# A list schedule that keeps one clock for all of SyncE's loads and stores, in a fused attention and SwiGLU kernel

## The chip, the cores and the metric

One core of a Trainium2 chip runs the whole kernel. The metric is device time in microseconds (us), the median of a few runs of the same program. TensorE does the matmuls, ScalarE (ACT) and VectorE (DVE) copy, round and add, GpSimd (POOL) takes some of that, and SyncE (SP) issues nearly all DMAs.

## The reference

Retention attention over 4 sequences of 768 tokens and 8 heads of 64, in blocks of 64 tokens with a carried state; then one SwiGLU layer over the 3072 token rows of 512:

```python
intra = (qb @ kb.T * Dmask) @ vb
inter = (qb * lam_pow) @ kv_state
out[:, :, sl] = intra + inter
kv_state = lam_block * kv_state + (kb * rev_pow).T @ vb
...
xn = x / sqrt(mean(x * x) + 1e-6) * rms_g
g = xn @ w_gate                       # 512 x 1536
return (silu(g) * (xn @ w_val)) @ w_out
```

All inputs and the output are float32. Matmuls of the SwiGLU part run as three float16 products each (high by high, low by high, high by low).

## The kernel before

The 3072 tokens are 6 groups m of 512, the 1536 hidden columns are 12 blocks f of 128, so there are 72 units (m, f), numbered u. The first 24 units (`classical`) are two plain products, gate and value, on weights that lie in the on-chip tile `w_half`. While they run, weights are converted to float16 pairs, sums of weight blocks are made and written out to `gw_kept` in DRAM. Units 24 to 71 (`strassen`) make the same two products out of seven smaller ones, and each of them first reads its weights back: `gv` (256 KB, three buffers) and `gw` (640 KB, two buffers). The two buffers of `gw` mean that a unit's load can't start before the last matmul on `gw` two loads earlier is over. In the names of the order below, `pa_3_1` and `pb_3_1` are the two accumulators of group 3, block 1, which is unit 37; `gw_37` is that unit's weights. A unit's result `sg` is stored in `h_kept`, read back later as `h`, and multiplied with the output weights (`o`, lines 924 and 1029). Attention of a coming group (`pa` at line 478, `po` at 539 and 550, on `qkv`) is woven in between.

Nothing of this order is written by hand. Each piece of work is a step with an engine, an estimated duration, a wished place `at`, and the names it reads and writes. `Plan.run` (lines 1110 to 1207) takes the steps one by one: it holds a clock per engine and picks the step that could start first. The recorded order is then the program order on each engine. `SHIFTS` (line 1691 on) is a table that moves the wished place of some steps, each named by its number. DMAs are steps too. Before, they were four separate engines with a clock each:

```python
ENGINES = ("PE", "ACT", "DVE", "POOL", "LD", "LO", "LH", "ST")
...
step("LO", 0.7, u - 1.6, load_val, u, f, r=[f"gk{f}:b"], w=[wv], new=[(wv, "gv")], lasts=1.8)
step("LO", 1.75, u - 1.59, load_others, u, f, r=[f"gk{f}:b", f"gk{f}:s", wv], w=[w], new=[(w, "gw")], lasts=1.8)
```

LD loads inputs, LO loads weights, LH loads rows and output weights, ST stores. A step of cost c and `lasts` l is taken to be finished c + l after its start. In the program all of these are DMAs of the one SyncE queue, in the order in which the plan placed them, and a DMA that must wait holds back those behind it.

Of the kernel before, what the change touches and what calls it, by code (L numbers as in the profile page):

```python
# [18 lines left out]
G = 512  # L19
# [3 lines left out]
def retention_swiglu_kernel(  # L23
# [754 lines left out]
    class Hidden:  # L778
# [38 lines left out]

        def keep(self, t):
            nc.scalar.copy(self.val_sums[:, t * HG : (t + 1) * HG], self.pa)  # L819

        def sum_val(self, t):
            v = self.val_sums[:, t * HG : (t + 1) * HG]
            nc.vector.tensor_add(v, self.pb, v)  # L823

        def keep_gate(self):
            self.sg = tmp.tile([P, G], F32, tag="t", name=f"sg_{self.m}_{self.f}")
            nc.scalar.copy(self.sg[:, HG:], self.pa)  # L827

        def sum_gate(self):
            nc.vector.tensor_add(self.sg[:, HG:], self.pb, self.sg[:, HG:])  # L830

        def silu_half(self, t):
            half = slice(t * HG, (t + 1) * HG)
            nc.scalar.activation(
                self.sg[:, half], self.sg[:, half] if t else self.pa, AF.Silu,
                scale=cg[:, self.f, 0:1],
            )

        def mul_sums(self, t=None):
            half = slice(0, G) if t is None else slice(t * HG, (t + 1) * HG)  # L840
# [102 lines left out]
    class Operands:  # L943
# [13 lines left out]
        def sums(self, part):  # L957
            if self.hs:
                (a11, a21), (a12, a22) = (
# [21 lines left out]
        def parts(self, n):  # L981
# [6 lines left out]
            if n == 0:  # L988
                return self.hs[0].sg[:, :HG], to[:, 0, 0], to[:, 0, 1]
# [70 lines left out]
    class Plan:  # L1060

        ENGINES = ("PE", "ACT", "DVE", "POOL", "LD", "LO", "LH", "ST")
# [41 lines left out]
        @staticmethod  # L1104
        def lag(a, b):
            if a == b:
                return 0.0 if a == "PE" else 0.03
            return 0.22 if a == "PE" else 0.1 if a in ("LD", "LO", "LH", "ST") else 0.06

        def run(self, horizon=1.3, reach=900):  # L1110
# [44 lines left out]
            while left:  # L1155
                for limit in (horizon, 99.0):
                    found = {e: [] for e in self.ENGINES}
                    for i in left[:reach]:
                        eng, _, at = steps[i][:3]
                        if at > progress + limit or eng in self.LOADS and found[eng]:  # L1160
# [6 lines left out]
                    found = {e: sorted(x for x in c if x[1] < 1e9) for e, c in found.items()}  # L1167
# [21 lines left out]
                start, eng, i = best  # L1189
                _, cost, at, _, _, r, w, new, lasts = steps[i]  # L1190
                clock[eng] = start + cost - self.NEXT.get(eng, 0.0)
# [91 lines left out]
    def out_weight_steps(j, at):  # L1283
# [3 lines left out]
        for i in range(2):  # L1287
            f = 2 * j + i
            step("LH", 1.4, at - 1.0 + 0.1 * i, load_o, f, w=[f"ro{f}"], new=[(f"ro{f}", "raw_o")], lasts=1.8)
# [10 lines left out]
        step("ST", 0.05, at + 0.65, o.keep, r=both, w=[f"wk{j}"], lasts=4.0)  # L1300
# [4 lines left out]
    def out_sum_steps(o, at):  # L1305
# [3 lines left out]
        step("LH", 1.4, at - 1.0, o.load, r=[f"wk{j}"], w=[b], new=[(b, "w")], lasts=1.8)  # L1309
# [5 lines left out]
    def block_steps(m, j, at, d):  # L1315
# [3 lines left out]
        step("LH", 1.4, at - 0.7, o.load, r=[f"hk{n}:0", f"hk{n}:1"], w=h, new=[(f"hp{n}", "w")], lasts=1.8)  # L1319
# [5 lines left out]
    def plain_rows_steps(m, at, length):  # L1325

        for i in range(2):
# [8 lines left out]
            for t in range(2):  # L1336
                key = f"ro{m}_{i}_{t}"
                step("ACT", 0.66, at + length * (i + 1) / 2 - 1, r.keep, t, r=[banks[t], "ik"], w=[key], new=[(key, "o")])
                step("ST", 0.05, at + length * (i + 1) / 2 - 1, r.send, t, r=[key], w=[f"sent{key}"], lasts=4.0)

    def sum_steps(f, at):
        s = WeightSums(f)
        both = [f"wg{f}", f"wv{f}", room_of(f)]
        step("ST", 0.1, at - 0.5, s.send_blocks, r=both, w=[f"gk{f}:b"], lasts=4.0)
# [9 lines left out]
        step("ST", 0.05, at + 1.3, s.send, r=[f"ws16_{f}"], w=[f"gk{f}:s"], lasts=4.0)  # L1354
# [198 lines left out]
    def strassen(u, h):  # L1553
# [8 lines left out]
        step("LO", 0.7, u - 1.6, load_val, u, f, r=[f"gk{f}:b"], w=[wv], new=[(wv, "gv")], lasts=1.8)  # L1562
        step("LO", 1.75, u - 1.59, load_others, u, f, r=[f"gk{f}:b", f"gk{f}:s", wv], w=[w], new=[(w, "gw")], lasts=1.8)
# [36 lines left out]
    def room_step(i, at):  # L1600
        step("ST", 0.0, at, late_room, i, new=[(f"late{i}", f"big{i}")], w=[f"late{i}:c{j}" for j in range(3)])

    def operand_steps(m, j, at, d):
# [7 lines left out]
        else:  # L1611
            h = [[f"hp{n}:{i}"] for i in range(2)]
            step("LH", 1.4, at - 0.7, o.load, r=[f"hk{n}:0", f"hk{n}:1"], w=[f"hp{n}:0", f"hp{n}:1"],
                 new=[(f"hp{n}", "w")], lasts=1.8)
# [19 lines left out]
    def rows_steps(m, at, length):  # L1634
# [5 lines left out]
        for k, n in enumerate(PHASES):  # L1640
# [13 lines left out]
            if n in to:  # L1654
# [3 lines left out]
                step("ST", 0.05, t, r.send, c, i, j, r=[f"late0:c{c}"], w=[f"sent{m}_{k}"], lasts=4.0)  # L1658
# [13 lines left out]
    def load_steps():  # L1672
        queue = [(1, 0), 1, 2, (1, 1), 3, (1, 2), 4, (1, 3), *range(5, NF)]
        queue += [(m, p) for m in range(2, NG) for p in range(NP)]
        for key in queue:
            if isinstance(key, tuple):
# [6 lines left out]
                step("LD", 2.8, -9, load_qkv, m, p, w=[f"{name}:{c}" for c in "qKkv"], new=[(name, "in")], lasts=1.8)  # L1683
            else:
                step("LD", 2.8, -9, load_gv, key, w=[f"gv{key}"], new=[(f"gv{key}", "in")], lasts=1.8)

    SHIFTS = {
# [252 lines left out]
```

## Time and profile before

| | us |
|---|---|
| median of 3 runs | 700.91 (698.31 to 705.19) |
| the profiled execution, own time | 704.38 |
| its span, first to last instruction | 702.6 |
| TensorE busy in the span | 653.7 (93%) |
| VectorE busy | 490.3 (70%) |
| mean granted clock of TensorE | 0.983 |

A busy TensorE is one that has a matmul in flight, not one at its full rate: the next matmul of a row starts before the last one has left. What a row costs is read from start to start, or from long merged rows. "Waited for" is idle time that ended when the thing named was done.

### The profile page before, as it was taken

The numbers are of one execution on the slowest core, as the hardware profiler recorded it, in microseconds if no ns is written. First come the engines' busy times: TensorE is split into PE (matmuls) and PEld (weight loads), VectorE is DVE, ScalarE is ACT, GpSimd is POOL, SyncE is SP. The second block draws the span as 40 slices with busy tenths as digits, with TensorE's granted clock in tenths as the row PEclk, the third lists the DMA queues.
The fourth block names the chain that finished last, engine by engine and source line by source line (L and its number), as shares of the span: only waits on it lengthen the run. The fifth ranks groups of instructions, "written<-read, shape, count | busy, mean of one in ns | idle before, by whom it ended". The sixth has DMA issues, their size and how long they took to land.

```text
span 702.6 us, 14209 instructions
## 1 busy us (share of the span) xinstructions
PE 653.7 (93%) x5667; PEld 494.4 (70%) x5667; DVE 490.3 (70%) x925; ACT 374.4 (53%) x696; POOL 136.7 (19%) x109
## 2 busy tenths in 40 slices
PE   8999999999979996998896989899999999999997
PEld 7865444445646764766674878788789888888886
DVE  6778977899899882776573738875665825854760
ACT  3669665965447551655564535564654424534630
POOL 2222600044553773120000301200121200000000
PEclk9999999999999998999998999999999999999999
DMA  8676499648676387757765554654864646442501
GB/s 321 220 248 244 168 366 350 230 148 269 237 258 210 123 293 274 244 167 251 253 219 199 191 208 166 215 183 140 275 209 127 196 145 210 169 140 76 195 16 46
DMA packets 58594, 144.06 MB, mean 205 GB/s; under 512 B 6176, under 2 KB 23072, under 8 KB 57120
## 3 DMA queue, kind: packets, MB, share of 16 engines
q1 hardware_dynamic: 58384, 142.64, 59.3%
q8 instruction: 44, 0.72, 0.4%
q10 hardware_dynamic: 144, 0.52, 0.3%
q14 instruction: 22, 0.18, 0.1%
HBM read 106.96 MB, written 36.18 MB: 204 GB/s over the span
## 4 chain that ended last, share of the span: by engine, by line
PE 62%; DMA 20%; DVE 9%; ACT 4%; issue 3%; SPq 1%; POOL 0%; DVEq 0%; ACTq 0%; POOLq 0%
PE o L1029 17%; PE pa L770 13%; PE pb L770 10%; DMA gw<-gw_kept 6%; PE pv L659 5%; PE pg L659 4%; DMA h_kept<-sg 4%; DMA h<-h_kept 4%; DMA gv<-gw_kept 3%; PE pa L478 2%; PE po L539 2%; PE o L924 2%; PE po L550 2%; PE pst L511 1%; PE pss L592 1%
## 5 line engine op out<-in xcount | busy, mean ns | idle before, releaser
L770 PEld LDWEIGHTS <-gw 128*128 128x128 f16 x1440 | 140.5, 99 | 49.1 <-DMA gw<-gw_kept 20.9
L1029 PE MATMUL o<-wo,late 128*128 128x256 f16 x1260 | 149.5, 273 | 0.0
L1029 PEld LDWEIGHTS <-late 128*128 128x128 f16 x1260 | 122.8, 98 | 15.5 <-issue 0.5
L659 PEld LDWEIGHTS <-w_half 128*128 128x128 f16 x576 | 54.1, 98 | 68.8 <-issue 6.2
L770 PE MATMUL pa<-tx,gw 128*128 128x256 f16 x576 | 79.5, 278 | 16.4 <-DMA gw<-gw_kept 15.3
L819 ACT COPY tx<-pa 128x256 f32<-128x256 f32 x96 | 35.4, 371 | 91.7 <-PE pa L770 82.2
L823 DVE TENSOR_TENSOR tx<-pb,tx 128x256 f32<-128x256 f32 x96 | 40.1, 421 | 48.7 <-PE pb L770 39.1
L770 PEld LDWEIGHTS <-gv 128*128 128x128 f16 x576 | 57.2, 101 | 20.2 <-DMA gv<-gw_kept 10.3
L659 PE MATMUL pv<-x,w_half 128*128 128x512 f16 x288 | 67.5, 379 | 2.8 <-DVE sg L851 1.6
L659 PE MATMUL pg<-x,w_half 128*128 128x512 f16 x288 | 67.9, 383 | 0.3 <-ACT w_half L440 0.3
L502 POOL TENSOR_TENSOR qkv<-qkv,pw 128x512 f32<-128x512 f32 x24 | 32.9, 1373 | 175.0 <-PE pa L478 162.6
L830 DVE TENSOR_TENSOR sg<-pb,sg 128x256 f32<-128x256 f32 x48 | 20.1, 422 | 50.7 <-ACT sg L827 49.3
L770 PE MATMUL pa<-x,gv 128*128 128x256 f16 x288 | 41.4, 282 | 9.6 <-DMA gv<-gw_kept 9.6
L999 DVE TENSOR_TENSOR late<-s,late 128x1024 f16<-128x1024 f32 x30 | 38.0, 1272 | 9.5 <-ACT late L995 9.5
L770 PE MATMUL pb<-tx,gw 128*128 128x256 f16 x288 | 40.3, 279 | 2.6 <-DMA gw<-gw_kept 2.1
L770 PE MATMUL pb<-x,gw 128*128 128x256 f16 x288 | 39.0, 272 | 2.7 <-DVE sg L830 2.6
L770 PE MATMUL pb<-x,gv 128*128 128x256 f16 x288 | 41.0, 281 | 0.0
L770 PE MATMUL pa<-x,gw 128*128 128x256 f16 x288 | 39.0, 272 | 0.0
L720 POOL TENSOR_TENSOR ws<-ws,ws 128x512 f16<-128x512 f32 x24 | 30.3, 1274 | 41.9 <-ACT ws L716 29.2
L995 ACT CAST late<-s 128x1024 f16<-128x1024 f32 x30 | 31.1, 1045 | 11.4 <-DVE s L979 8.1
L924 PE MATMUL o<-wo,early 128*128 128x512 f16 x144 | 35.6, 382 | 0.0
L498 DVE TENSOR_TENSOR a<-pa,mask 128x512 f32<-128x512 f32 x48 | 31.4, 684 | 5.7 <-PE pa L478 3.6
(147 smaller groups left out, 1071.2 us busy)
## 6 DMA issues: line engine op xcount, KB each, us to landing
gw<-gw_kept SPq DMA_DIRECT2D x48, 640.0 KB, 4.5
qkv<-in_qkv_dram SPq DMA_DIRECT2D x47, 512.0 KB, 6.3
h<-h_kept SPq DMA_DIRECT2D x30, 512.0 KB, 4.5
gv<-gw_kept SPq DMA_DIRECT2D x48, 256.0 KB, 4.9
raw_gv<-in_weights_dram SPq DMA_DIRECT2D x11, 1024.0 KB, 6.6
h_kept<-sg SPq DMA_DIRECT2D x60, 128.0 KB, 4.9
h_kept<-sg SPq DMA_DIRECT2D x30, 256.0 KB, 4.7
raw_o<-in_weights_dram SPq DMA_DIRECT2D x24, 256.0 KB, 4.3
```

Source lines behind the costliest of these rows:

```text
L498: nc.vector.tensor_mul(self.a[:, j], self.pa[j], decay)
L502: eng.tensor_mul(self.qT, self.qT, pw[:, p : p + 1, :].broadcast_to([P, GC, P]))
L659: nc.tensor.matmul(ps, w[:, kk, :], x[:, kk, :], start=i == kk == 0, stop=i == 2 and kk == NK - 1,)
L720: eng.tensor_sub(self.to[:, c, 1], self.t[:, c], self.to[:, c, 0])
L770: nc.tensor.matmul(ps, w(ow, k), x(ox, k), start=first and i == k == 0, stop=i == 2 and k == 1, skip_group_check=True,)
L819: nc.scalar.copy(self.val_sums[:, t * HG : (t + 1) * HG], self.pa)
L823: nc.vector.tensor_add(v, self.pb, v)
L830: nc.vector.tensor_add(self.sg[:, HG:], self.pb, self.sg[:, HG:])
L924: nc.tensor.matmul(self.banks[t], h[:, oh, t * P : (t + 1) * P], wo[:, j, 3 + 2 * k : 5 + 2 * k, ow], start=j == k == i == 0, stop=j == HA ...
L995: nc.scalar.copy(hi, of)
L999: eng.tensor_sub(lo, of, hi)
L1029: nc.tensor.matmul(bank[:, t], ops[:, oh, t * P : (t + 1) * P], w[:, ow], start=n in (1, 2, 5) and q == t == i == 0, stop=q == HALF - 1 an ...
```

## The change

Work, tiles and arithmetic stay. Three things differ.

First, the plan: LD, LO, LH and ST share one clock, `SP`, and their costs and `lasts` are larger. A load of `gw` was finished 1.75 + 1.8 = 3.55 us after its start and is now finished after 2.4 + 2.8 = 5.2, a load of `gv` after 1.0 + 2.8 = 3.8 in place of 2.5; stores, which cost 0.05, now hold the clock for 0.8 to 1.55. Steps that only open a tile go to a clock of their own, `ROOM`, where they cost nothing.

Second, `SHIFTS` is another table (one line of each stands below).

Third, for units 24 and up the two halves of `sg` with an even f are kept in the order in which they are stored, so that `keep_h` is one DMA of 256 KB where it was two of 128 KB. The program has 359 DMA issues on SyncE where it had 377.

```diff
-        ENGINES = ("PE", "ACT", "DVE", "POOL", "LD", "LO", "LH", "ST")
+        ENGINES = ("PE", "ACT", "DVE", "POOL", "SP", "ROOM")
+
+        SP = ("LD", "LO", "LH", "ST")
...
+        def half(self, t):
+
+            t = t if self.f % 2 else 1 - t
+            return slice(t * HG, (t + 1) * HG)
...
-            if self.f % 2:
-                nc.sync.dma_start(to[:, 1], self.sg)
+            if self.f % 2 or self.u >= 2 * NF:
+                nc.sync.dma_start(to[:, self.f % 2], self.sg)
...
-        @staticmethod
-        def lag(a, b):
+        def lag(self, a, b):
+            if a in self.SP:
+                return 0.1
...
-                            found[eng].append((at, t, i))
-                        elif eng in self.LOADS:
-                            found[eng].append((at, 1e9, i))
+                            found["SP" if eng in self.SP else eng].append((at, t, i))
+                        if eng in self.LOADS:
+                            seen.add(eng)
...
-                clock[eng] = start + cost - self.NEXT.get(eng, 0.0)
+                if cost:
+                    clock[unit] = start + cost - self.NEXT.get(eng, 0.0)
...
-        step("ST", 0.05, u - 1, h.keep_h, r=[f"sg{u}:0", f"sg{u}:1", f"sg{u}"], w=[f"hk{h.m}_{h.f // 2}:{h.f % 2}"],
-             lasts=4.0)
+        step("ST", 0.8, u - 1, h.keep_h, r=[f"sg{u}:0", f"sg{u}:1", f"sg{u}"], w=[f"hk{h.m}_{h.f // 2}:{h.f % 2}"],
+             lasts=2.0)
...
-        step("LO", 0.7, u - 1.6, load_val, u, f, r=[f"gk{f}:b"], w=[wv], new=[(wv, "gv")], lasts=1.8)
-        step("LO", 1.75, u - 1.59, load_others, u, f, r=[f"gk{f}:b", f"gk{f}:s", wv], w=[w], new=[(w, "gw")], lasts=1.8)
+        step("LO", 1.0, u - 1.6, load_val, u, f, r=[f"gk{f}:b"], w=[wv], new=[(wv, "gv")], lasts=2.8)
+        step("LO", 2.4, u - 1.59, load_others, u, f, r=[f"gk{f}:b", f"gk{f}:s", wv], w=[w], new=[(w, "gw")], lasts=2.8)
...
-                step("LD", 2.8, -9, load_qkv, m, p, w=[f"{name}:{c}" for c in "qKkv"], new=[(name, "in")], lasts=1.8)
+                step("LD", 3.7, -9, load_qkv, m, p, w=[f"{name}:{c}" for c in "qKkv"], new=[(name, "in")], lasts=2.8)
...
-        2709: 6.123, 2715: 5.968,
...
+        2637: 8.777, 2641: 4.085, 2656: 1.098, 2675: -2.059, 2701: 1.816, 2716: 1.22,
```

The order changes nearly everywhere on all five engines. Two places show what the prediction rests on.

TensorE, from the last use of the buffer that `gw_39` needs to the first matmul on `gw_39` (unit 39 is group 3, block 3). Before, that buffer was `gw_37`'s; between any two rows that are shown stand more matmuls of the same kind, six to a product:

```order
L770 MATMUL pb_3_1_3796<-x_3_2440,gw_37_3681 128x256
...
L770 MATMUL pa_3_0_3763<-x_3_2440,gw_36_3751 128x256
...
L770 MATMUL pb_3_0_3778<-x_3_2440,gw_36_3751 128x256
...
L770 MATMUL pa_3_2_3966<-x_3_2440,gv_38_3804 128x256
...
L770 MATMUL pb_3_2_3974<-x_3_2440,gv_38_3804 128x256
...
L770 MATMUL pa_3_3_3985<-x_3_2440,gv_39_3708 128x256
...
L770 MATMUL pb_3_3_3996<-x_3_2440,gv_39_3708 128x256
...
L770 MATMUL pa_3_3_3985<-tx_0_2178,gw_39_3954 128x256
```

In the change the buffer was `gw_35`'s, and the load stands in the queue right behind that of `qkv_4_2`, which needs `po_4_0` finished (line 550):

```order
L770 MATMUL pb_2_11_3642<-x_2_1918,gw_35_3651 128x256
...
L550 MATMUL po_4_0_3784<-qkv_4_0_2995,state_170 64x128 x6
...
L770 MATMUL pb_3_1_3815<-x_3_2376,gv_37_3631 128x256
...
L770 MATMUL pa_3_2_3828<-x_3_2376,gv_38_3773 128x256
...
L770 MATMUL pa_3_1_3757<-tx_0_2101,gw_37_3739 128x256
...
L1034 MATMUL o_1_1_3862<-wo_178,late0_3578 128x256
...
L770 MATMUL pb_3_1_3815<-x_3_2376,gw_37_3739 128x256
...
L1034 MATMUL o_1_2_3920<-wo_178,late0_3578 128x256
...
L770 MATMUL pa_3_3_3964<-x_3_2376,gv_39_3789 128x256
...
L770 MATMUL pa_3_3_3964<-tx_0_2101,gw_39_3879 128x256
```

Before, 36 matmuls of 128x256 lie between the release and the use. In the change the rest of unit 37, products of `o` and attention's scores of the next pair have moved in between.

SyncE, in the stretch of the queue with the loads of units 38 to 41. Before:

```order
L736 DMA gw_39_3954<-gw_kept3_100 128x2560
L736 DMA gw_38_3981<-gw_kept2_99 128x2560
L862 DMA h_kept3_0_133<-sg_3_0_3928 128x256 x2
L858 DMA h_kept3_0_133<-sg_3_1_3845 128x512
L731 DMA gv_41_4006<-gw_kept5_102 128x1024
L951 DMA h_1_5_4049<-h_kept1_5_126 128x1024
L736 DMA gw_41_4074<-gw_kept5_102 128x2560
L96 DMA qkv_4_3_4093<-in_qkv_dram 128x1024 x2
L731 DMA gv_40_4097<-gw_kept4_101 128x1024
```

And in the change:

```order
L736 DMA gw_39_3879<-gw_kept3_100 128x2560
L96 DMA qkv_4_3_3916<-in_qkv_dram 128x1024 x2
L956 DMA h_1_4_3961<-h_kept1_4_125 128x1024
L864 DMA h_kept3_0_133<-sg_3_1_3905 128x512
L736 DMA gw_38_4000<-gw_kept2_99 128x2560
L731 DMA gv_40_4032<-gw_kept4_101 128x1024
L956 DMA h_1_5_4043<-h_kept1_5_126 128x1024
L864 DMA h_kept3_0_133<-sg_3_0_3702 128x512
```

`gv_40` stood right behind the 1 MB load of `qkv_4_3`; now three rows, a load of `gw` among them, lie between the two, and the store of `sg_3_0` is one row of 128x512 without the mark x2.

## Rows read from the trace of the kernel before

**Rows 1.** The page: span, then busy time of engines with share and instruction count.

```profile
span 702.6 us, 14209 instructions
...
PE 653.7 (93%) x5667; PEld 494.4 (70%) x5667; DVE 490.3 (70%) x925; ACT 374.4 (53%) x696; POOL 136.7 (19%) x109
```

**Rows 2.** Stretches of 50 us: busy time by engine, granted clock, DMA share, GB/s.

```profile
150.00:200.00 50.00, 46.09 (x363) 25.49 (x362) 46.12 (x83) 24.21 (x36) 25.15 (x21) 0.98 0.72 242
200.00:250.00 50.00, 46.63 (x416) 32.39 (x414) 44.52 (x80) 30.26 (x50) 28.42 (x21) 0.98 0.57 202
...
350.00:400.00 50.00, 41.90 (x400) 34.68 (x400) 32.40 (x60) 25.83 (x49) 4.01 (x3) 0.93 0.58 194
...
500.00:550.00 50.00, 49.27 (x498) 42.37 (x496) 33.19 (x62) 27.89 (x57) 9.01 (x6) 1.00 0.63 206
```

**Rows 3.** What TensorE waited for: us in total, times, longest us.

```profile
PE pa L770 <- DMA gw<-gw_kept: 15.3, 9, 5.8
PE pa L770 <- DMA gv<-gw_kept: 9.6, 2, 6.5
...
PE pb L770 <- DMA gw<-gw_kept: 2.1, 1, 2.1
```

**Rows 4.** Timeline of TensorE, 354 to 384 us: start, length, what, idle before.

```profile
359.68 0.82 PE L770 MATMUL pb<-x,gv 128*128 128x256 f16 x6
361.85 0.83 PE L770 MATMUL pa<-tx,gw 128*128 128x256 f16 x6 [1.35 <-DMA gw<-gw_kept]
...
371.19 0.57 PE L511 MATMUL pst<-qkv 128*64 128x64 f32 x12
378.22 1.46 PE L770 MATMUL pa<-x,gv 128*128 128x256 f16 x6 [6.46 <-DMA gv<-gw_kept]
```

**Rows 5.** Timeline of SyncE, 354 to 384 us: DMA issues, start and length.

```profile
368.62 0.81 SPq L96 DMA_DIRECT2D qkv<-in_qkv_dram  x2
369.48 0.42 SPq L731 DMA_DIRECT2D gv<-gw_kept  x1
```

**Rows 6.** Tile gw: its loads.

```profile
DMA to landing us min/median/max: 3.7/4.5/9.1
```

**Rows 7.** Tile gv: its loads.

```profile
DMA to landing us min/median/max: 2.7/4.9/9.0
```

**Rows 8.** Tile qkv: its loads.

```profile
DMA to landing us min/median/max: 3.8/6.3/9.5
```

**Rows 9.** Four stretches in which the granted clock was half: columns as in rows 2.

```profile
266.60:273.40 6.80, 4.50 (x20) 3.00 (x21) 0.03 (x1) 0.74 (x2) 0.00 (x0) 0.50 0.89 345
341.70:345.10 3.40, 3.40 (x19) 2.39 (x16) 0.42 (x1) 2.28 (x5) 0.00 (x0) 0.51 1.02 373
375.80:382.60 6.80, 4.38 (x21) 3.14 (x22) 1.46 (x5) 1.10 (x4) 0.00 (x0) 0.50 0.26 96
413.30:416.70 3.40, 2.78 (x14) 1.99 (x15) 0.00 (x0) 0.37 (x1) 0.00 (x0) 0.50 0.10 39
sum 20.40, PE 15.06 PEld 10.52 DVE 1.92 ACT 4.50 POOL 0.00; mean PE 3.76 PEld 2.63 DVE 0.48 ACT 1.12 POOL 0.00
```

**Rows 10.** Chain that ended last: start, length, piece.

```profile
157.44 2.59 PE pg L659 x12
...
197.15 7.22 DMA h_kept<-sg
204.39 3.66 DMA h<-h_kept
...
213.90 6.11 DMA h<-h_kept
...
672.51 26.21 PE o L1029 x240
```

**Rows 11.** What SyncE's DMA queue waited for: us in total, times, longest us.

```profile
SPq L1048 <- DVE late L1042: 67.4, 11, 16.7
```

More of the change, by code (lines that the diff above doesn't have):

```diff
@@ L816, in add @@
             )
+        def half(self, t):
+            t = t if self.f % 2 else 1 - t
+            return slice(t * HG, (t + 1) * HG)
         def keep(self, t):
-            nc.scalar.copy(self.val_sums[:, t * HG : (t + 1) * HG], self.pa)
+            nc.scalar.copy(self.val_sums[:, self.half(t)], self.pa)
         def sum_val(self, t):
-            v = self.val_sums[:, t * HG : (t + 1) * HG]
+            v = self.val_sums[:, self.half(t)]
             nc.vector.tensor_add(v, self.pb, v)
@@ L826, in keep_gate @@
             self.sg = tmp.tile([P, G], F32, tag="t", name=f"sg_{self.m}_{self.f}")
-            nc.scalar.copy(self.sg[:, HG:], self.pa)
+            nc.scalar.copy(self.sg[:, self.half(1)], self.pa)
         def sum_gate(self):
-            nc.vector.tensor_add(self.sg[:, HG:], self.pb, self.sg[:, HG:])
+            g = self.sg[:, self.half(1)]
+            nc.vector.tensor_add(g, self.pb, g)
         def silu_half(self, t):
-            half = slice(t * HG, (t + 1) * HG)
+            half = self.half(t)
             nc.scalar.activation(
@@ L839, in mul_sums @@
         def mul_sums(self, t=None):
-            half = slice(0, G) if t is None else slice(t * HG, (t + 1) * HG)
+            half = slice(0, G) if t is None else self.half(t)
             sg = self.sg[:, half]
@@ L1157, in run @@
                     found = {e: [] for e in self.ENGINES}
+                    seen = set()
                     for i in left[:reach]:
                         eng, _, at = steps[i][:3]
-                        if at > progress + limit or eng in self.LOADS and found[eng]:
+                        if at > progress + limit or eng in seen:
                             continue
@@ L1163, in run @@
                         if t is not None:
[L1164 to L1167 removed]
+                            found["SP" if eng in self.SP else eng].append((at, t, i))
+                        if eng in self.LOADS:
+                            seen.add(eng)
+                    found = {e: sorted(c) for e, c in found.items()}
                     if any(found.values()):
@@ L1188, in run @@
                         best = start, eng, pick[2]
-                start, eng, i = best
-                _, cost, at, _, _, r, w, new, lasts = steps[i]
-                clock[eng] = start + cost - self.NEXT.get(eng, 0.0)
+                start, unit, i = best
+                eng, cost, at, _, _, r, w, new, lasts = steps[i]
+                if cost:
+                    clock[unit] = start + cost - self.NEXT.get(eng, 0.0)
                 end[i] = start + cost + lasts
@@ L1288, in out_weight_steps @@
             f = 2 * j + i
-            step("LH", 1.4, at - 1.0 + 0.1 * i, load_o, f, w=[f"ro{f}"], new=[(f"ro{f}", "raw_o")], lasts=1.8)
+            step("LH", 1.9, at - 1.0 + 0.1 * i, load_o, f, w=[f"ro{f}"], new=[(f"ro{f}", "raw_o")], lasts=2.8)
             step("ACT", 0.67, at + 0.2 * i, o.lift, i, r=[f"ro{f}"], w=[f"{b}:{i}"],
@@ L1299, in out_weight_steps @@
         w = f"wo{j}"
-        step("ST", 0.05, at + 0.65, o.keep, r=both, w=[f"wk{j}"], lasts=4.0)
+        step("ST", 1.55, at + 0.65, o.keep, r=both, w=[f"wk{j}"], lasts=2.0)
         step("ACT", 1.1, at + 0.65, o.high, 0, r=both, w=[f"{w}:0", f"{w}:1"])
@@ L1308, in out_sum_steps @@
         b, w, t = f"wog{j}", f"wo{j}:1", f"wt{j}"
-        step("LH", 1.4, at - 1.0, o.load, r=[f"wk{j}"], w=[b], new=[(b, "w")], lasts=1.8)
+        step("LH", 1.9, at - 1.0, o.load, r=[f"wk{j}"], w=[b], new=[(b, "w")], lasts=2.8)
         step("DVE", 0.84, at, o.sums, 0, r=[b], w=[t], new=[(t, "raw_o")])
@@ L1318, in block_steps @@
         h = [f"hp{n}:{i}" for i in range(2)]
-        step("LH", 1.4, at - 0.7, o.load, r=[f"hk{n}:0", f"hk{n}:1"], w=h, new=[(f"hp{n}", "w")], lasts=1.8)
+        step("LH", 1.9, at - 0.7, o.load, r=[f"hk{n}:0", f"hk{n}:1"], w=h, new=[(f"hp{n}", "w")], lasts=2.8)
         for i in range(2):
@@ L1338, in plain_rows_steps @@
                 step("ACT", 0.66, at + length * (i + 1) / 2 - 1, r.keep, t, r=[banks[t], "ik"], w=[key], new=[(key, "o")])
-                step("ST", 0.05, at + length * (i + 1) / 2 - 1, r.send, t, r=[key], w=[f"sent{key}"], lasts=4.0)
+                step("ST", 0.8, at + length * (i + 1) / 2 - 1, r.send, t, r=[key], w=[f"sent{key}"], lasts=2.0)
     def sum_steps(f, at):
@@ L1343, in sum_steps @@
         both = [f"wg{f}", f"wv{f}", room_of(f)]
-        step("ST", 0.1, at - 0.5, s.send_blocks, r=both, w=[f"gk{f}:b"], lasts=4.0)
+        step("ST", 1.2, at - 0.5, s.send_blocks, r=both, w=[f"gk{f}:b"], lasts=2.0)
         for i in range(2):
@@ L1353, in sum_steps @@
             step("POOL", 1.15, at + 1.1 + 0.05 * i, s.low, i, r=[f"ws{f}"], w=[f"ws16_{f}"])
-        step("ST", 0.05, at + 1.3, s.send, r=[f"ws16_{f}"], w=[f"gk{f}:s"], lasts=4.0)
+        step("ST", 1.55, at + 1.3, s.send, r=[f"ws16_{f}"], w=[f"gk{f}:s"], lasts=2.0)
     def classical(u, h, columns=None):
@@ L1600, in room_step @@
     def room_step(i, at):
-        step("ST", 0.0, at, late_room, i, new=[(f"late{i}", f"big{i}")], w=[f"late{i}:c{j}" for j in range(3)])
+        step("ROOM", 0.0, at, late_room, i, new=[(f"late{i}", f"big{i}")], w=[f"late{i}:c{j}" for j in range(3)])
     def operand_steps(m, j, at, d):
@@ L1612, in operand_steps @@
             h = [[f"hp{n}:{i}"] for i in range(2)]
-            step("LH", 1.4, at - 0.7, o.load, r=[f"hk{n}:0", f"hk{n}:1"], w=[f"hp{n}:0", f"hp{n}:1"],
-                 new=[(f"hp{n}", "w")], lasts=1.8)
+            step("LH", 1.9, at - 0.7, o.load, r=[f"hk{n}:0", f"hk{n}:1"], w=[f"hp{n}:0", f"hp{n}:1"],
+                 new=[(f"hp{n}", "w")], lasts=2.8)
             if m <= UNSCALED:
@@ L1657, in rows_steps @@
                     step("DVE", 0.74, t, r.sum, c, r=[names[False], "ik"], w=[f"late0:c{c}"])
-                step("ST", 0.05, t, r.send, c, i, j, r=[f"late0:c{c}"], w=[f"sent{m}_{k}"], lasts=4.0)
+                step("ST", 0.8, t, r.send, c, i, j, r=[f"late0:c{c}"], w=[f"sent{m}_{k}"], lasts=2.0)
     FACTORS = 23
@@ L1682, in load_steps @@
                 name = f"q{m}_{p}"
-                step("LD", 2.8, -9, load_qkv, m, p, w=[f"{name}:{c}" for c in "qKkv"], new=[(name, "in")], lasts=1.8)
+                step("LD", 3.7, -9, load_qkv, m, p, w=[f"{name}:{c}" for c in "qKkv"], new=[(name, "in")], lasts=2.8)
             else:
-                step("LD", 2.8, -9, load_gv, key, w=[f"gv{key}"], new=[(f"gv{key}", "in")], lasts=1.8)
+                step("LD", 3.7, -9, load_gv, key, w=[f"gv{key}"], new=[(f"gv{key}", "in")], lasts=2.8)
     SHIFTS = {
[97 rows of a table removed]
[125 rows of a table added]
     }
@@ L1840, in retention_swiglu_kernel @@
                     norm_steps(m + 1, u, 0.2)
-        step("ST", 0.0, START[0] - 3, early_room, new=[("early", "big0")], w=["early:"])
+        step("ROOM", 0.0, START[0] - 3, early_room, new=[("early", "big0")], w=["early:"])
         for m in range(PLAIN):
```

6 lines of the change are left out of this document (3 added, 3 removed), and 221 rows, old and new, of the table SHIFTS.

## The prediction

> **What bounds the kernel now.** I read the page first: TensorE has a matmul in flight in 653.7 of 702.6 us, VectorE is busy in 490.3 [rows 1]. So TensorE is the engine to follow, and a gain must come from its idle time or from time in which it runs below its rate. The windows of 50 us say where that is [rows 2]: it is idle for 3.9 and 3.4 us between 150 and 250 us, for 8.1 between 350 and 400, and hardly at all at 500 to 550. Between 150 and 250 VectorE is busy in 46.12 and 44.52 of 50 us, so there it is close to being the bound; from 350 on it has a third of its time free.
>
> Third, what TensorE waits for [rows 3]. The waits for the weight loads of the units with seven products stand out: 15.3 + 9.6 + 2.1 = **27.0 us** in 12 waits, the longest 5.8 and 6.5. The timeline shows one of each kind [rows 4]: 1.35 us for `gw` at 361.85, and 6.46 us for `gv` at 378.22. The queue shows why the second is so long [rows 5]: `gv` is issued at 369.48, directly behind the two halves of a `qkv` load of 1 MB that started at 368.62, and lands only when TensorE goes on, 8.7 us later.
>
> Fourth, the clock. After the long waits stand four stretches at 0.50 of the granted clock, the lower of the two levels, 1.2 GHz for 2.4 [rows 9]: six matmuls took 1.46 us behind the wait of 6.46 and 0.83 behind the one of 1.35 [rows 4]. In these 20.40 us TensorE was busy for 15.06, and half of that, **7.5 us**, would not have been needed at the upper level. The Trainium skill (TensorE: Matmul & The Clock Gate, Terms) counts the penalty as the whole throttled time by one minus the share of the clock. By that the four stretches cost 10.2 us, because it counts the idle part of them too; the sum below goes by the busy part.
>
> **What the change moves, and the price of each part.** A 128x256 matmul costs 26.21 / 240 = 0.109 us in a long row, a 128x512 one 2.59 / 12 = 0.216 [rows 10]. With these prices I count in the order the TensorE work between what a load must wait for (the free buffer, and all that the queue's rows ahead of it wait for) and the first matmul on the load; call it the load's room. For `gw_39` before it is 36 matmuls, 3.9 us; in the change 12.8. The queue needs 4.5 us from issue to landing for `gw`, 3.7 at best and 9.1 at worst [rows 6], and 4.9, 2.7 and 9.0 for `gv` [rows 7]. A room of 3.9 us is thus nearly always too small, and that is what the old plan gave: it took 3.55 us for granted. Over all 48 units the rooms of `gw` are:
>
> - before: 8 at 3.9, 25 under 6.0, the middle one 5.9;
> - in the change: none under 5.7, 7 under 6.0, the middle one 7.9.
>
> For `gv` the least grows from 3.0 to 5.2, and those under 6.0 fall from 4 to 2. The loads of `qkv`, which land after 6.3 us in the middle [rows 8], had 6 rooms under 6.0 (least 3.0) and now none under 7.2. No kind of load has lost its room.
>
> *Waits for `gw` and `gv`*: 27.0 us go. What is left? Upper bound: each old wait stays, less the growth of the tight rooms, 2.0 for `gw` (3.9 to 5.9) and 2.2 for `gv` (3.0 to 5.2). 5.8 becomes 3.8, the eight others of that row, 1.2 each, vanish, 2.1 becomes 0.1, 6.5 becomes 4.3 and 3.1 becomes 0.9: 9.1 us. Lower bound: that, scaled by the tight loads of both kinds, 9 for 29: 2.8 us. I take 6.0, the middle, since the worst landings (9.1, 9.0) are beyond the new middle rooms.
>
> *Half speed*: 7.5 us go. If the two longest waits stay as in the upper bound, their stretches stay, (4.50 + 4.38) / 2 = 4.4 us [rows 9]; if not, nothing. I take 2.4.
>
> *The stage of 150 to 250 us.* Here TensorE's chain runs through stores and loads of the hidden rows: `h_kept` 7.22 us, `h` 3.66, `h` again 6.11 [rows 10]. The least room of an `h` load grows from 5.9 to 9.0. The first matmul on a `gv` load also comes after 9.6 us less TensorE work (199.3 for 208.9), which only moves that work behind it. VectorE stays nearly full, so of the 7.3 us that TensorE idles here I take 3.0 as gained; bounds 0 and 7.3.
>
> *Stores of `sg`*: 18 DMA issues fewer, at about 0.4 us each on the queue [rows 5], 7 us of SyncE. They are covered: SyncE is waiting for others in far more than that, 67.4 us for the output rows alone [rows 11]. Nothing for TensorE. The new halves of `sg` change which columns are written, not the size of a step: nothing. `ROOM` issues nothing. Filler matmuls in the first stage are 43 for 51; they stand in waits, so nothing (at most 2 us).
>
> Sum: 704.4 - 27.0 - 7.5 + 6.0 + 2.4 - 3.0 = 675.3 us for the profiled execution's own time. That execution stands 3.5 us above the median of its runs, so I scale by 700.91 / 704.38: **672 us**, 4.1% faster.
>
> **The rivals.**
>
> *The load waits are only a cover (688 us).* With TensorE no longer held up, VectorE and ScalarE meet it with less lead. The old waits gave them time to catch up; for this speaks VectorE's 46.12 of 50 [rows 2], against it the third of its time that is free from 350 us on, where most of the load waits are. If half of the net gain on loads (27.0 + 7.5 - 6.0 - 2.4 = 26.1) comes back as waits for them and the early stage gives nothing, 704.4 - 13.0 = 691.4, scaled 688.
>
> *All of it goes (659 us).* No load is late, the half-speed stretches vanish, and the early stage loses its 7.3 us too: 704.4 - 34.5 - 7.3 = 662.6, scaled 659. The worst landings speak against it.
>
> *No change (701 us).* The loads could land later just because they are issued earlier, into the same 1 MB transfers, so that more room buys nothing. Rows 6 speak against it: nearly all landings lie between 3.7 and 9.1, and it is the room that was short. Here belongs a rule of the Trainium skill (DMA: Bandwidth & Descriptors, Anatomy of one DMA, given for the gpsimd path): 2.0 us and the bytes by 436 GB/s. By it a `gw` load of 640 KB takes 3.5 us, the old plan's 3.55 was right, a room of 3.9 held every load, and the change could give nothing at all, 701 us. The trace disagrees, 4.5 in the middle [rows 6]. That a larger plan cost moved nothing, so that the change would not do what it says, is out: the rooms in the order have grown.
>
> *Slower (715 us).* One row of SyncE holds back all behind it. A store of output rows waits 67.4 / 11 = 6.1 us for VectorE [rows 11]. My rooms count TensorE's work only: if VectorE is late, a `gw` load behind such a store is issued 6.1 us later, the middle room leaves 7.9 - 4.5 = 3.4, and TensorE waits 2.7 us. Ten such loads eat up the gain of 27.0; with 16 of them and the old load waits and half speed gone it is 704.4 - 29.1 + 43.2 = 718.5, scaled 715. For it: in the new order 44 of the 96 loads of `gv` and `gw` stand right behind a store, in the old one 36. Against: the old order had nearly as many, and its waits came where rooms were small, as at 361.85.
>
> **How the numbers follow.** Forecast (662 to 684): 0.52. Half comes back (684 to 694): 0.19. All goes (under 662): 0.15. No change: 0.08. Slower: 0.06. The three runs shown lie within 1%, so I count 1% as what can be told from no change. Faster by more than that, under 693.9: 0.52 + 0.19 + 0.15 = 0.86; within 1%: 0.08; slower: 0.06. The range reaches from just below the case in which all goes, 657, to 694, the edge of the one in which half comes back; about 0.05 lies below it and 0.14 above. The forecast's own range is 662 to 684.
>
> **What would show it.** In the list of TensorE's waits, `gw` and `gv` together between 3 and 9 us instead of 27.0. Stretches at half clock behind load waits: two or fewer, with the window of 350 to 400 above 0.93. The landing times of `gw` about as before, 4.5 in the middle: then the room did it; if they fall to 3.7, the transfers got faster and the step is another. In the windows from 150 to 250, TensorE's idle time 7.3 or less. I am wrong if the waits for loads go and the time doesn't, with new rows of VectorE or ScalarE in TensorE's list; or if those for loads stay with rooms of 6 to 8 us, which would say that the queue, not the buffers, made them late.

## The result, and the profile after

The changed kernel took **654.48 us** (median of 4 runs, 654.07 to 655.37), the kernel before 703.05 us beside it (4 runs, 698.31 to 708.28): ratio 0.9309, 95% interval 0.9237 to 0.9382, so 6.9% faster. Forecast were 672 us, with a range from 657 to 694. The sign was right, and the time lies 2.5 us below the range, on the far side of the rival "All of it goes" (659 us, with a chance of 0.15), which is the case that came nearest. The profiled execution took 655.37 us with a span of 653.6.

First the page, the lines that answer to [rows 1]: span, busy time of the engines, and the chain that ended last by engine.

```profile
span 653.6 us, 14094 instructions
...
PE 640.0 (98%) x5651; PEld 487.2 (75%) x5651; DVE 482.1 (74%) x925; ACT 375.2 (57%) x696; POOL 136.2 (21%) x109
...
PE 79%; DVE 12%; ACT 4%; DMA 3%; issue 2%; POOL 0%; SPq 0%; DVEq 0%; ACTq 0%
```

Read the two page lines as a subtraction. The span fell by 49.0 us. TensorE's idle time (span less busy) fell from 702.6 - 653.7 = 48.9 to 653.6 - 640.0 = 13.6, that is by 35.3; its busy time fell by 13.7. So most of the gain is waits that are gone; the rest is taken apart term by term further below. DMA now holds 3% of the chain, where it held 20%.

TensorE's waits, the answer to [rows 3]; this is the head of the list (us in total, times, longest):

```profile
PE pg L659 <- DVE sg L857: 1.7, 1, 1.7
PE unread L144 <- POOL ident masks.py:199: 1.5, 1, 1.5
PE po L539 <- ACT sq L573: 1.4, 1, 1.4
PE pa L770 <- ACT x L632: 1.2, 1, 1.2
```

No row of the whole list has a DMA as the releaser. The 27.0 us in 12 waits for `gw` and `gv` are not smaller, they are gone. The `gw` loads themselves are no faster. Tile `gw`, which answers to [rows 6]:

```profile
DMA to landing us min/median/max: 3.7/4.5/9.2
```

That is the line of before but for 0.1 at the end. For `gv` it is 2.5/4.1/7.0, so those loads do land sooner, 0.8 us in the middle and 2.0 at the worst; for `qkv` it is 3.5/5.8/10.6. The windows that answer to [rows 2], and the one stretch left at half clock (same columns):

```profile
150.00:200.00 50.00, 47.24 (x370) 26.21 (x370) 44.57 (x87) 27.02 (x41) 26.10 (x22) 1.00 0.75 252
200.00:250.00 50.00, 48.29 (x421) 35.90 (x418) 42.54 (x71) 29.86 (x55) 33.49 (x24) 0.97 0.77 247
350.00:400.00 50.00, 50.00 (x492) 43.64 (x491) 33.31 (x61) 31.21 (x57) 4.66 (x3) 1.00 0.73 244
500.00:550.00 50.00, 50.00 (x459) 44.78 (x457) 32.11 (x58) 24.89 (x49) 3.59 (x2) 1.00 0.61 199
...
217.30:220.70 3.40, 3.40 (x32) 2.41 (x34) 3.33 (x6) 1.17 (x3) 2.25 (x2) 0.50 0.79 226
```

From 350 to 400 us TensorE was busy in 41.90 of 50 us and is now busy in all of them, at the upper clock (1.00); the same window holds later work now, since the order runs ahead. All four half-clock stretches of [rows 9] are gone. VectorE's busy time in that window rose by 0.9 us only, and TensorE waits for nothing there: the time that the old waits gave VectorE to catch up was not needed.

### The profile page after: what moved, and what is told of

The parts are those of the page before. It is cut to its first block, busy times and chain, and to the rows that moved or that the text cites. A ratio compares the mean times of both kernels' runs of the same rounds, so it can differ in the third digit from the quotient of the medians.

```text
span 653.6 us, 14094 instructions
## 1 busy us (share of the span) xinstructions
PE 640.0 (98%) x5651; PEld 487.2 (75%) x5651; DVE 482.1 (74%) x925; ACT 375.2 (57%) x696; POOL 136.2 (21%) x109
## 2 busy tenths in 40 slices
DMA packets 56001, 144.05 MB, mean 220 GB/s; under 512 B 5888, under 2 KB 18176, under 8 KB 54528
## 4 chain that ended last, share of the span: by engine, by line
PE 79%; DVE 12%; ACT 4%; DMA 3%; issue 2%; POOL 0%; SPq 0%; DVEq 0%; ACTq 0%
PE o L1034 21%; PE pa L770 19%; PE pb L770 14%; PE pv L659 4%; PE pg L659 4%; PE o L929 4%; PE pa L478 3%; PE po L539 3%; PE po L550 2%; PE pst L511 2%; PE pss L592 1%; PE pr L621 1%; DMA qkv<-in_qkv_dram 1%; DVE wo_f L217 1%; DMA gw_kept<-ws 1%
## 5 line engine op out<-in xcount | busy, mean ns | idle before, releaser
L1034 PE MATMUL o<-wo,late 128*128 128x256 f16 x1260 | 152.8, 273 | 0.0
L824 ACT COPY tx<-pa 128x256 f32<-128x256 f32 x96 | 35.3, 372 | 67.1 <-PE pa L770 54.2
L836 DVE TENSOR_TENSOR sg<-pb,sg 128x256 f32<-128x256 f32 x48 | 20.2, 422 | 37.1 <-ACT sg L832 35.3
L770 PE MATMUL pa<-x,gv 128*128 128x256 f16 x288 | 39.6, 272 | 1.4 <-ACT x L632 1.2
L770 PE MATMUL pb<-x,gv 128*128 128x256 f16 x288 | 39.3, 273 | 0.0
L1044 ACT ACTIVATE late<-o,ik 128x512 f32<-128x512 f32 x20 | 13.7, 686 | 41.3 <-PE o L1034 41.3
L699 POOL TENSOR_TENSOR r<-w_half 128x512 f32<-128x512 f16 x24 | 34.6, 1460 | 11.1 <-DVE ws L712 7.9
```

The costliest lines, as they stand in the source:

```text
L699: nc.gpsimd.tensor_add(self.r[:, i], w[:, 0], w[:, 1])
L770: nc.tensor.matmul(ps, w(ow, k), x(ox, k), start=first and i == k == 0, stop=i == 2 and k == 1, skip_group_check=True,)
L824: nc.scalar.copy(self.val_sums[:, self.half(t)], self.pa)
L836: nc.vector.tensor_add(g, self.pb, g)
L1034: nc.tensor.matmul(bank[:, t], ops[:, oh, t * P : (t + 1) * P], w[:, ow], start=n in (1, 2, 5) and q == t == i == 0, stop=q == HALF - 1 an ...
```

## The experiments

Twelve kernels were run, each beside the kernel before. "Before + edit" and "change + edit" say which of the two was edited.

**1. Shorter `gw` loads (before + edit).** If short rooms cause the waits, a faster load must remove them with the order left alone.

```
-        nc.sync.dma_start(t, gw_kept[f][:, V_END:])
+        nc.sync.dma_start(t[:, : G_END - V_END], gw_kept[f][:, V_END:G_END])
...
-                return lambda o, k: sums[:, j, o, cols[k]]
+                return lambda o, k: g1[:, o, cols[k]]
```

> Kernel before, its order unchanged, but each gw load brings 128 KB in place of 640 KB: the four blocks of weight sums are left out and the gate block is used in their place, so TensorE does the same matmuls. Theory A (rooms: a load was late because its landing took longer than the TensorE work between the free buffer and the use): a landing falls from 4.5 us in the middle to about 3, under the smallest room of 3.9; the waits for gw (15.3 + 2.1 us) go to under 2, the half-speed stretches at 267 and 413 us go, and the time falls by 18 to 28 us to 675 to 685. Theory B (the waits are only a cover, VectorE and ScalarE are as late as the loads): waits for gw become waits for VectorE and ScalarE, the time falls by less than 9 us, to 694 or more.

Measured: 683.5 us beside 703.25, ratio 0.9732 (0.9685 to 0.978), 19.8 us less. Tile `gw` of this kernel, its loads:

```profile
DMA to landing us min/median/max: 2.0/2.5/7.9
```

And what its TensorE waited for (us in total, times, longest):

```profile
PE pa L770 <- DMA gv<-gw_kept: 4.9, 2, 3.5
PE pa L770 <- DMA gw<-gw_kept: 4.4, 2, 4.0
...
PE pb L770 <- DMA gw<-gw_kept: 1.4, 1, 1.4
```

Those for `gw` fell from 17.4 to 5.8 us in the unchanged order (under 2 were expected; the longest landing is still 7.9 us, and the longest wait 4.0). `gv`, not edited, lands sooner too, after 3.5 us in the middle where it was 4.9. So most of these waits were a matter of landing time against room, as the prediction had it.

**2. Both loads shorter (before + edit).** As 1, and `gv` at half its bytes.

```
-        nc.sync.dma_start(v, gw_kept[f][:, :V_END])
+        nc.sync.dma_start(v[:, : V_END // 2], gw_kept[f][:, : V_END // 2])
...
-                (lambda o, k: v[:, o, cols[k]], given(0, first)),
+                (lambda o, k: v[:, 0, cols[k]], given(0, first)),
```

> Kernel before, order unchanged, gw loads of 128 KB as in the experiment with short gw loads, and gv loads of 128 KB too: half of the value block is left out and the other half used twice. If all the loss behind 240 us is late loads and what they bring with them (half clock), the waits for gv (4.9 us left in that experiment) and gw (4.4 left) go nearly to nothing and the time falls by 8 to 15 us against its 683.5, to 668 to 675. The rest against the change's 654.5 would then be the stage before, 5 us, and waits for VectorE and ScalarE. If other things than loads bound that part, under 5 us less than 683.5.

Measured: 679.81 us beside 703.87, ratio 0.9646 (0.961 to 0.9683): 24.1 us less, only 4.3 more than experiment 1 gave. `gv` now lands after 3.1 us in the middle, and yet TensorE's waits in this kernel show single ones of 4.5 and 3.0 us:

```profile
PE pa L770 <- DMA gw<-gw_kept: 5.0, 2, 4.5
PE pa L770 <- DMA gv<-gw_kept: 4.0, 2, 3.0
PE pb L770 <- DVE sg L830: 2.9, 4, 1.4
...
PE pb L770 <- DMA gw<-gw_kept: 1.3, 1, 1.3
```

What follows: the few longest landings come only in part from a load's own bytes. The 8 to 15 us expected did not come, but 10.3 us of waits for loads are left, so this run does not tell whether something else bounds that part. And 25 us (679.81 less 654.48) of the change's gain are not to be had by making these loads light.

**3. What made one landing long (before + edit).** `gv_40` stood behind the 1 MB load of `qkv_4_3` and landed 8.7 us after its issue [rows 4, 5]. Here it goes ahead of it.

```
+        order.insert(at[load_val, (40, 4)], order.pop(at[load_qkv, (4, 3)]))
```

> Kernel before, with two neighbours of SyncE's queue exchanged: the gv load of unit 40 goes ahead of the 1 MB load of qkv_4_3, behind which it stood; nothing else in the order moves. Its room grows from 3.0 to 4.4 us. Theory F (a long landing is the bytes and waits of the queue rows just ahead, not chance): it lands 4 to 5.5 us after its issue in place of 8.7, TensorE waits for it under 1.5 us in place of 6.46, the half-speed stretch behind goes too, and the time falls by 6 to 9 us, to about 695 to 697 where before is 703. Theory G (landings spread by chance, as the prediction took them): it lands about as late, the wait falls by the 1.4 us of room, and the time by 1 to 2 us.

Measured: 701.81 us (12 runs) beside 703.87, ratio 0.996 (0.9932 to 0.9988): 2.8 us by the ratio, 2.1 by the medians, less than half of what was expected. `gv_40` landed 4.2 us after its issue, and the wait of 6.46 is gone. The timeline of this kernel's TensorE at the place (start, length, what, idle before):

```profile
360.34 0.83 PE L770 MATMUL pa<-tx,gw 128*128 128x256 f16 x6 [1.13 <-DMA gw<-gw_kept]
...
376.73 0.33 PE L511 MATMUL pst<-qkv 128*64 128x64 f32 x2 [2.65 <-ACT qkv L488]
377.40 0.56 PE L511 MATMUL pst<-qkv 128*64 128x64 f32 x10 [0.34 <-ACT qkv L488]
```

And the chain of waits through the same stretch of it (start, length, piece):

```profile
367.90 8.19 DMA qkv<-in_qkv_dram
376.09 0.02 issue
...
376.17 0.51 ACT qkv L488
```

Now it is the `qkv` load that TensorE waits for, 8.19 us after its issue, by way of ScalarE, and 2.65 + 0.34 us of the 6.46 are given back. The exchange did not make that load slower. Tile `qkv` in the kernel before, the two halves of this load alone (window 368.5 to 369.3 us):

```profile
DMA to landing us min/median/max: 7.6/8.0/8.4
```

The same load in this kernel (window 367.4 to 368.2 us):

```profile
DMA to landing us min/median/max: 7.3/7.8/8.2
```

It was as late before, but TensorE was then still waiting for `gv_40`. So the landing of `gv_40` depended on its place behind this load, and one exchange uncovers the next late load behind the first: an order needs room for both. Why the gain is smaller still than these numbers leave stays open.

**4. The round trip of the hidden rows (before + edit).** The chain of before runs through `h_kept` and `h` [rows 10]. Here six `h` loads read an input, so that they wait for no store.

```
-            nc.sync.dma_start(self.t, h_kept[self.m, self.j])
+            nc.sync.dma_start(self.t, qkv[0, 0, :, 0:2])
```

> Kernel before, but the six loads of the hidden rows of group 0 read a block of the input of the same size in place of the stored rows, so they no longer wait for the stores (the output of group 0 is not the reference's). Theory C (the early stage lost its time to the round trip of the hidden rows: 7.22 us of a store and 3.66 and 6.11 of loads in the chain): the time falls by 3 to 9 us, to 694 to 700, with less idle time of TensorE between 200 and 260 us. Theory D (the order of VectorE's work in that stage, which this kernel keeps): within 2 us of the kernel before.

Measured: 705.62 us, ratio 1.0024 (0.999 to 1.0058). The theory that these trips hold the time falls. That a transfer stands in the chain that ended last did not mean that taking its wait away would shorten the whole.

**5. Two stores for one (change + edit).** The 18 DMA issues that the change saves, put back.

```
-                nc.sync.dma_start(to[:, self.f % 2], self.sg)
+                if self.f % 2:
+                    nc.sync.dma_start(to[:, 1], self.sg)
+                else:
+                    for i in range(2):
+                        half = slice(i * HG, (i + 1) * HG)
+                        nc.sync.dma_start(to[:, 0, half], self.sg[:, half])
```

> Changed kernel, but the stores of sg with an even f are two DMAs of 128 KB again, 18 issues more. If the queue's issue time is covered, as the prediction's sum has it, within 3 us of the change (652 to 658). If SyncE's row is tight, 18 x 0.4 = 7 us slower, 661 or more.

Measured: 655.44 us (655.03 to 655.86), ratio to before 0.9335 (0.9297 to 0.9374), 1.0 us above the change. The stores are covered, as the prediction had it.

**6. Every `gw` load twice (change + edit).** Meant to make the landing longer in the new order.

```
         nc.sync.dma_start(t, gw_kept[f][:, V_END:])
+        nc.sync.dma_start(t, gw_kept[f][:, V_END:])
```

> Changed kernel, each gw load issued twice into the same buffer, the order otherwise unchanged. The second copy should land 2 to 3.5 us later, so 6.5 to 8 us after the release where it was 4.5. Theory A: against the rooms of the change (14 of 48 under 7.0 us, 22 under 8.0) that leaves 5 us of late landings at 6.5, 12 at 7.0, 20 at 7.5 and 30 at 8.0; with the spread of landings and some half-speed stretches the time grows by 12 to 40 us to 667 to 695. Theory B: the order has slack elsewhere and takes it, under 6 us.

Measured: 766.29 us, ratio 1.0925 (1.0862 to 1.0988), 112 us more than the change and far above what any theory gave. The queue shows why the test was cruder than meant. What SyncE's queue waited for in this kernel:

```profile
SPq L737 <- DMA gw<-gw_kept: 241.2, 48, 9.2
```

And its TensorE:

```profile
PE pa L771 <- DMA gw<-gw_kept: 53.5, 26, 4.3
PE pa L771 <- DMA gv<-gw_kept: 18.5, 6, 5.7
PE pb L771 <- DMA gw<-gw_kept: 8.5, 4, 2.7
```

The second copy into a buffer has to wait on SyncE until the first has landed, 241.2 / 48 = 5.0 us each time, and all rows of the queue behind it wait too: `gv`, whose own loads were not touched, goes from no wait to 18.5 us. How much of the 112 us is the waiting row and how much the added bytes was not separated, and the run does not show how much room a load of twice the bytes would need.

**7. The plan without its table.** After the costs, the plan reads a table of shifts (`SHIFTS`) that moves single steps. Four kernels leave it empty: the old plan (7a), the old plan with the change's transfer times (7b), the change's single row with the old times (7c), and the change's plan (7d).

```
-    SHIFTS = {
...
-    }
+    SHIFTS = {}
```

> Kernel before with an empty table of shifts: the old plan by itself. Its order has 145 filler matmuls where before has 51, and 6 of 48 rooms of gw under 4.6 us, the least 3.9. Slower than before by 20 to 60 us, since the plan itself sees more idle time of TensorE; waits of TensorE for gw and gv of 8 us or more.

> The old plan with four clocks and no shifts, but with the changed kernel's costs and landing times of loads and stores. No room of gw under 5.0 (139 fillers). Theory H (the longer landing times alone make the rooms, and the rooms make the time): its waits for gw and gv are under 3 us and it is 5 to 20 us faster than the old plan with old costs. Theory I (one clock for SyncE is what counts): waits about as in the old plan, within 5 us of it.

> The changed plan with one clock for SyncE and no shifts, but with the old costs and landing times. Its least room of gw is again 3.9 (6 under 4.6, 158 fillers). Theory H: waits for loads as in the old plan without shifts, within 5 us of its time. Theory I: loads that stand behind others no longer come late; waits under 3 us and 5 to 20 us faster.

> The changed kernel with an empty table of shifts: one clock and the new costs. Rooms of gw not under 5.2; 161 fillers where the change has 43. Waits for loads under 3 us; faster than the old plan without shifts by 5 to 20 us, but slower than the change by 30 us or more, since the table of shifts took away idle time that the plan itself sees.

Measured: 7a **694.27** (ratio 0.9863, 0.9812 to 0.9914), 7b 693.69 (0.9856, 0.98 to 0.9913), 7c 698.23 (0.9914, 0.9882 to 0.9946), 7d **694.22** us (0.9862, 0.9803 to 0.992). I had expected the old plan to be 20 to 60 us slower without its table. It is 1.4% faster. And all four lie within 5 us: neither the single row nor the new transfer times gain anything by themselves, and the 5 to 20 us that theories H and I promised are both absent. TensorE's waits for loads are small in 7a and 7d. Of its list in 7a, the head and the first row for a DMA:

```profile
PE pa L770 <- ACT tx L819: 5.7, 4, 3.1
...
PE pa L770 <- DMA gv<-gw_kept: 1.6, 1, 1.6
```

The same two rows in 7d:

```profile
PE pa L770 <- ACT tx L824: 2.1, 1, 2.1
...
PE pa L770 <- DMA gv<-gw_kept: 1.1, 2, 0.6
```

And the rows for a DMA in 7b, under the longer transfer times:

```profile
PE pa L770 <- DMA gw<-gw_kept: 4.7, 4, 1.8
...
PE pa L770 <- DMA gv<-gw_kept: 2.4, 3, 1.1
```

This limits what rooms alone can tell. 7a has 6 of 48 `gw` rooms under 4.6 us, the least 3.9, and waited 1.8 us for `gw` and `gv`, where I had expected 8 or more; 7b has no `gw` room under 5.0 and waited 7.1. The six tight loads of 7a landed 3.7 to 4.8 us after their issue. So it also counts which landings fall on the tight rooms.

**8. The tables crossed.** The old table under the change's plan, and the change's table under the old plan; the edit exchanges the lists.

> The changed kernel's plan (one row for SyncE, new transfer times) with the table of shifts of the kernel before. Theory J, a table is worth something only under the plan that it was made for: its order has 25.5 us more TensorE work than the kernel before (651.9 for 626.4, filler matmuls), gw rooms from 3.3 us up with 15 of 48 under 6.0, so load waits of 5 to 15 us come back and the time is 695 to 715 us, no better than with no table at all (694.2). Theory K, the new plan's rule makes the rooms whatever the table: under 675 us.

> The kernel before with the changed kernel's table of shifts, under the old plan (four rows for loads and stores, short transfer times). Theory J: 644.3 us of TensorE work, and gw rooms like those of the kernel before (25 of 48 under 6.0, least 3.3), so load waits of 20 to 35 us and 700 to 725 us. Theory L, the new table by itself holds the gain, because it puts the loads earlier: under 675 us.

Measured: 719.56 (ratio 1.0235, 1.0212 to 1.0259) and 744.74 us (1.0585, 1.0563 to 1.0607). Both are slower than before, and they lie 4.6 and 19.7 us above the tops of theory J's ranges; K and L, under 675, fall. The waits for loads came as J had them, 10.4 and 21.1 us; the second also waits for ScalarE. TensorE's waits under the old plan with the new table:

```profile
PE pa L770 <- DMA gw<-gw_kept: 15.5, 9, 4.5
PE pa L770 <- ACT sg L827: 11.3, 3, 6.1
PE pa L770 <- ACT tx L819: 8.5, 3, 5.5
```

The medians together:

| | no table | old table | new table |
|---|---|---|---|
| old plan | 694.27 | 703.05 | 744.74 |
| new plan | 694.22 | 719.56 | 654.48 |

The gain sits in one corner. The new rule without a table gives nothing, the new table without the rule does harm, and each table is better under its own plan than under the other.

To see what a table does, split the time into the TensorE work of the order (an estimate: every matmul at its rate in the traces, fillers included) and the lag, by which TensorE's start of a matmul in the trace is behind that work. The lag is read where 600 us of work are done:

| | work | lag | span |
|---|---|---|---|
| old plan, no table | 648.0 | 41.7 | 695.5 |
| old plan, old table | 626.4 | 72.2 | 702.6 |
| old plan, new table | 644.3 | 92.2 | 742.0 |
| new plan, no table | 651.7 | 32.8 | 690.5 |
| new plan, old table | 651.9 | 59.5 | 716.2 |
| new plan, new table | 624.5 | 25.2 | 653.6 |

The work differs by the fillers, matmuls on `unread` that the plan puts where it expects TensorE to wait. The groups of instructions by line count them (busy time, mean ns, idle before). In the change's plan without its table, 7d:

```profile
L144 PE MATMUL unread<-ident 128*128 128x128 f32 x322 | 41.0, 285 | 1.5 <-POOL ident masks.py:199 1.5
```

In the change with it:

```profile
L144 PE MATMUL unread<-ident 128*128 128x128 f32 x86 | 12.9, 306 | 1.5 <-POOL ident masks.py:199 1.5
```

So both tables took planned waits out, 21.6 and 27.2 us of work, each under its own plan. The old one paid for it with 30.5 us of lag, against 25.2 us more of TensorE's waits for loads in its trace (27.0 for the 1.8 of 7a); the new one paid nothing, the lag fell by 7.6. That the old one's price comes of the 3.55 us at which the plan counted a `gw` load, so that rooms of 3.9 looked enough, is argued and not shown.

## Why the prediction was wrong

**What held.** The mechanism, from the rooms to the waits: experiment 1 takes away two thirds of the `gw` waits by shorter landings, the change removes them by longer rooms, with `gw` landings as they were (4.5 us in the middle). The stores cost nothing (experiment 5). The old load waits were no cover for VectorE or ScalarE: the "half comes back" rival (688) falls, since TensorE's waits that are not for loads went down with the others. "No change" falls. By the rule of the Trainium skill that stood beside it (DMA: Bandwidth & Descriptors, Anatomy of one DMA), which the page gives for the gpsimd path while these loads are SyncE's, a `gw` load would land in an estimated 3.5 us. The traces have 4.5 in the middle in both kernels. "Slower" falls: SyncE's rows do wait longer for VectorE. Of the waits of SyncE's queue in the change:

```profile
SPq L1053 <- DVE late L1047: 86.5, 13, 16.8
```

That is 86.5 us for the 67.4 of [rows 11], and still no load behind these stores is late for TensorE.

**What failed.** Of the 19.9 us by which the sum was short (49.0 less 29.1), 8.4 come from one step, and the rest, to within 1 us, from terms that the sum put at nothing. The step is "Upper bound: each old wait stays, less the growth of the tight rooms", and with it the 6.0 us taken for waits left and the 2.4 for half speed left; measured are 0 and 0. It treated a landing of 8 or 9 us as a thing that strikes a load at random and would strike as often in the new order. It does not. Experiment 3 turns the 8.7 us of `gv_40` into 4.2 by a different place in the queue. And in the traces, the 29 loads of `gw` and `gv` with rooms under 7 us took up to 9.7 us in the kernel before, from the moment at which all that they must wait for was done to their landing (4.9 in the middle; 8 of them over 6.2), while the 21 such loads of the change took at most 6.2 (4.2 in the middle). Its long landings, up to 9.2 for `gw`, fall on loads with room for them; the closest calls came 0.6 us before their first use. Not one of the 96 loads was waited for. The views for this were at hand: the order of the change gives what stands ahead of each load in the queue, and [rows 5] had shown what a 1 MB neighbour does. That the order keeps long landings off the tight loads rests on this one exchange and on the comparison of two traces; it was not tested by itself.

The terms put at nothing are the waits that are not for loads outside the early stage, the fillers, and what a wait costs beyond its idle time: 5.6, 3.7 and some 3 us, as the list shows. The first two had rows at hand and were left out without a reason that holds.

**The sum, term by term.** Forecast were 24.0 us less idle time (27.0 - 6.0 + 3.0) and 5.1 less busy time (7.5 - 2.4), 29.1 in all; measured are 35.3 and 13.7, 49.0 in all.

- Waits for loads left: 6.0 forecast, 0 measured. The lower bound of 2.8 was too high as well.
- Waits that are not for loads: the trace of before has 17.7 us of them in its list (44.7 less the 27.0), the change 9.1. That is 8.6 gone where I took 3.0, and only for the stage from 150 to 250 us. I left out the rest. Two rows of TensorE's waits in the kernel before show some of it:

```profile
PE pb L770 <- DVE sg L830: 2.6, 3, 1.4
...
PE pst L511 <- DVE a L498: 1.5, 1, 1.5
```

  In the change the first is 0.6 and the second 0.3. Not all of them shrank: the wait of 1.7 for `sg` at the head of the change's list answers to one of 1.6 before. With these two terms the idle time comes to 24.0 + 6.0 + 5.6 = 35.6 for the 35.3 measured.
- Half speed left: 2.4 forecast, 0 behind load waits. The stretch at 217.3 us above stands behind waits of 1.2 us for ScalarE and 0.3 for VectorE; before, too, there was such a fifth one, at 198.3, behind a wait of 2.9 us for VectorE.
- Fillers: put at "nothing (at most 2 us)", but their busy time fell by 3.7 (16.6 in the kernel before, 12.9 above).
- Not in the sum: what a wait costs beyond its idle time. Six matmuls behind a wait took 0.83 us [rows 4] where the rate gives 6 x 0.109 = 0.655; 0.17 us for each of 18 waits fewer (30 before, 12 now) is about 3 us, an estimate made after the result. The busy time then comes to 5.1 + 2.4 + 3.7 + 3.1 = 14.3 for the 13.7 measured.

For the stage from 150 to 250 us the size came out: idle time of 7.3 before and 4.5 now, 2.8 for the 3.0 forecast. That was luck in part, since 3.0 was a choice between bounds of 0 and 7.3, and the two windows do not hold the same work. The rival "All of it goes" was right that no load is late, and wrong on this stage, of which it took all 7.3.

**Readings of mine that need mending.** The rooms of `gw` before, counted to the first matmul on the load as the prediction says, are 23 under 6.0 with 7.2 in the middle, not 25 and 5.9, and 8.7 in the middle in the change, not 7.9; the 8 at 3.9 and the least rooms hold, and so does the sum, but for the scaling behind the lower bound of 2.8. For `gv` one room in the change is under 6.0, not two. In the upper bound the "eight others" stand at their mean of 1.2 us; one of them was 3.1, so that bound is 10.2 by its own rule. The sum of "Slower" takes off 29.1, the whole forecast gain, where its words make it 34.5: 713.1, scaled 710. And the forecast speaks of the plan's transfer times as what gives the rooms. Experiments 7 and 8 show that these times alone give nothing; the order that they allow a table to make does.

**What stays open.** Which half of the new rule the table needs, the single row or the transfer times: without a table neither moves the time, and no table made under one of them alone was run. Experiment 2 puts 24.1 of the 49 us on the size of these loads, and [rows 3, 9] 34.5 on their waits and the slow clock behind them. No experiment gave more than those 24.1 us; what lies beyond them is accounted for by the traces alone. How far the smaller waits for VectorE and ScalarE fell because of that, or because of the table's other shifts, was not separated.

## What to carry to other kernels

Measure a load's room, the work between the moment it can start and its first use, against its landing time in the trace; waits sit where the room is under the landing, and the remedy can be either. The least rooms alone do not rank two orders (7a and 7b). Before pricing what remains in a new order, look at what stands just ahead of each tight load: a long landing can belong to a large neighbour (8.7 us behind it, 4.2 ahead of it), and here the new order had none on a tight load, so the lower bound of what is left is zero. A table tuned against a planner belongs to the planner's costs: change the costs and it must be made again, and under wrong costs it can be worse than none (703.05 against 694.27 here).

## What the runs showed of the hardware

- The landing of one and the same 256 KB load depended on its place in the queue: 8.7 us behind a 1 MB load, 4.2 ahead of it. The 1 MB load was no slower for it: its later half landed after 8.4 us before and after 8.2 then.
- A second DMA into a buffer that one was still filling had to wait at the queue for that one's landing, 5.0 us each in 48 loads, and later rows of that queue with it: TensorE waited 18.5 us for untouched `gv` loads. The kernel took 112 us more, with 175.52 MB moved for 144.05.
- At 128 KB for 640 the `gw` landing fell from 4.5 to 2.5 us in the middle, and the worst only from 9.1 to 7.9.
